# Loads of x re-ordered and spread over the run, a third buffer for the transposed softmax, and a new list order in an attention-and-MLP kernel

## The chip, the cores and the metric

The kernel runs on one core of one Trainium2 chip. The metric is the device time of a run in microseconds (us). Engines are named as in the profile: PE (TensorE), DVE (VectorE), ACT (ScalarE), POOL (GpSimd, which here mostly issues DMAs that convert FP32 to FP16 on the way) and SP (SyncE, which issues plain and transposing DMAs).

## What is computed

For each of 8 batches and 8 heads, 512 tokens x and 32 state vectors of width 64 attend to each other. Then all 8 x 544 rows go through an MLP whose activation is s·relu(h)² + b.

```python
scores = x @ state^T / 8;  a  = softmax(scores);   xread = a @ state     # 512 rows
scores2 = state @ x^T / 8; a2 = softmax(scores2);  sread = a2 @ x        #  32 rows
rows = concat(xread, sread) of all heads            # (8*544, 512)
r = relu(rows @ w_in)                               # (.., 2048)
out = (s*r*r + b) @ w_out                           # (.., 512)
```

All inputs and the output are FP32.

## The kernel before, in words

**Softmax.** Per batch, state and x are needed transposed (`stT`, `xT`). T holds the scores of all heads (`T_mm`, 16 small matmuls into two PSUM banks). ACT takes their exponential E (`E_exp`, L540). A matmul with a block matrix of ones gives the sums D over the 32 states (`D_mm`), and ACT forms 1/D as a logarithm and an exponential (L559, L566). The product a = E/D (L573) is the weight of xread. For sread, E is scaled by the row sums (`a2_mul`, L612), transposed by two DMAs to `aT` (`aT_dma`, L621) and multiplied with x (`V_mm`); the result goes through another transposing DMA to `srdT` (`sr_dma`, L651).

**First MLP matmul.** xread itself is never formed. M = stateᵀ-blocks times w_in is built per batch in four chunks of 512 columns (`M_mm`, eight small matmuls into two banks each, then two casts, L310 on ACT or L312 on DVE), and h = aᵀM gives 128 of the 2048 hidden rows in two matmuls of 512 columns (`h_mm`). There are 16 such f per batch. ReLU is on ACT (L779) or DVE (L771), the square on DVE (L785). h has two PSUM buffers.

**Second MLP matmul.** Batch 0 uses o = g·w_out directly, in 512-wide matmuls. Batches 1 to 7 use a Strassen-like scheme of seven products per batch in 256-wide matmuls, for which DVE forms differences of g (`pd`, L801 to L812) and of w_out (`u`, L860 to L866). DVE scales each product into an output tile (L928, L1024), and POOL or SP stores it (L934, L1036). The sread rows of all batches come last (`h_sr`, `osr`).

**Transposes.** Batches 0 to 2 (`NB_HW = 3`) transpose x and the state on PE with an identity, and DVE copies the result from PSUM. Batches 3 to 7 use transposing DMAs on SP for x (`dma_xT`, L462, four per batch) and one for the state (L446).

**Loads.** x of batch 0 comes as FP32 in four parts through SP (L248) and is cast by ACT. Everything else big is loaded on POOL with conversion, in the order of the string `SEQ` (L403), where wi and wo are quarters of w_in and w_out:

```python
SEQ = "wi0 x1 wi1 stf1 wo0 wi2 wo1 wi3 wo2 wo3 x2 sb x3 x4 x5"
```

x1 to x5 are whole batches. x of batches 6 and 7 comes in quarters of two heads each, with an earliest planned time from 62 us on. The first load waits for the identity through a small copy on POOL (`gate`, L402). A load issues only when the one eight places earlier has landed.

**Order.** No scheduler of the compiler is used. `Plan` holds a list of all operations, with an engine (or two to choose from) and a cost, a key, what each needs, and buffers. `Plan.order` walks through planned time and takes, on each free engine, the ready operation of the lowest key; that fixes the order of instructions on each engine. The keys are formed from the constants in `K`. While nothing is ready on PE, filler matmuls on the tile `warm` are placed until 14 us. `after` is an earliest planned time only: on the chip an instruction waits for what it needs and for those before it on its engine, not for a time.

Of the kernel before, what the change touches and what calls it, by code (L numbers as in the profile page):

```python
# [13 lines left out]
class Plan:  # L14
# [13 lines left out]
    def order(self, filler, fill_until, ready):  # L28
# [25 lines left out]
        mode, channel, log, now, done_n = False, 7.0, [], 0.0, 0  # L54
        times = []

# [15 lines left out]
        while done_n < len(ops):  # L72
            for e in free_at:
# [29 lines left out]
                if best is None:  # L103
                    fill = 0.43 if now < 7.0 else 0.22
                    if e == "PE" and now < fill_until and not any(since[i] < now + fill for i in cand[e]):
                        free_at[e] = now + fill
                        times.append(free_at[e])
                        log.append((now, len(log), "PE", filler, "warm", free_at[e]))
                    continue
# [13 lines left out]
                if land is not None:  # L123
                    kind, span = land
                    if kind == "load":
                        done = max(channel, end + 2.0) + span
                        channel = max(channel, done)
                    elif kind == "tp" and now < channel - 4.0:
                        end, done = now + 4.0, now + 9.0
                    else:  # L130
                        done = end + span
# [25 lines left out]
def kernel(  # L157
# [66 lines left out]
    nc.vector.memset(warm, 0.0)  # L224
    ident16 = konst.tile([P, P], FP16, name="ident16")
    ident_dr = nc.inline_tensor(np.eye(P, dtype=np.float16), name="ident_const")
    bones_np = np.kron(np.eye(4), np.ones((Ns, Ns))).astype(np.float16)
    bones16 = konst.tile([P, P], FP16, name="bones16")
    bones_dr = nc.inline_tensor(bones_np, name="bones_const")
    st_v = state.rearrange("b (g hf) j d -> (hf j) (b g) d", g=NG)  # L230
    NB_HW = 3
    stf = konst.tile([P, NG, D], FP32, name="stf")
    stf1 = konst.tile([P, (NB_HW - 1) * NG, D], FP32, name="stf1")
    stf2 = konst.tile([P, (B - NB_HW) * NG, D], FP32, name="stf2")
    xf = [upool.tile([P, H // 2, SCH * D], FP32, name=f"xf_{i}", tag="u") for i in range(2)]
    x0_v = x[0].rearrange("h (q c) d -> q h (c d)", q=P)

    def xf_part(i):
        return xf[i // 2][:, 2 * (i % 2) : 2 * (i % 2) + 2]
# [6 lines left out]
    nc.scalar.dma_start(stf, st_v[:, 0:NG, :])  # L246
    for i in range(4):
        nc.sync.dma_start(xf_part(i), xf_heads(x0_v, i))  # L248
    nc.scalar.dma_start(bones16, bones_dr.ap())
# [5 lines left out]
    s_bc = konst.tile([P, 1], FP32, name="s_bc")  # L255
    b_bc = konst.tile([P, 1], FP32, name="b_bc")
# [6 lines left out]
    st16 = konst.tile([P, B * NG, 2, D], FP16, name="st16")  # L263
    xn = {}
    xn[0] = xpool.tile([P, H, SCH, D], FP16, name="xn_0", tag="xn")

    def cast_x0(eng, i):
        eng(
            xf_heads(xn[0], i).rearrange("p h c d -> p h (c d)"),
            xf_part(i),  # L270
        )

    def cast_st(eng, src, n0, n):
        for k in range(2):
            eng.tensor_copy(st16[:, n0 : n0 + n, k, :], src)

    def late_dma(dst, src):


        nc.gpsimd.memset(dst, 0.0)  # L280
        nc.sync.dma_start(dst, src)

    K = dict(
        h1=4.4, hs=0.6, M0=-5.6, M1=0.9, T1=0.0, x2=24.6, T2=23.7, D2=27.2, M2=35.3, V0=27.7, V1=21.3, u=12.3,
        us=5.1, pd1=12.5, o0=13.1, o2=23.0, w=26.2, r=0.5, T=-9.8, D=3.1, Mb=6.4, V=8.6, S=3.6, S0=0.1, E=-0.5,
        L=-6.2, a4=-4.7, Mc=1.5, pd=13.4, solo=2.0, hsr=-4.1, Ssr=0.0,
# [3 lines left out]
    stTd = konst.tile([P, (B - NB_HW) * NG, P], FP16, name="stTd")  # L290
# [17 lines left out]
    def copy_on(e, dst, src):  # L308
        if e == "ACT":
            nc.scalar.copy(dst, src)  # L310
        else:
# [5 lines left out]
            "a40": 2, "a41": 2, "M": 2, "aT": 2, "a20": 2, "a21": 2, "sr": 4, "g": 8, "pd": 7,  # L317
# [16 lines left out]
    def cast_x0(i):  # L334
        def fn(e):
            copy_on(
                e,
                xf_heads(xn[0], i).rearrange("p h c d -> p h (c d)"),
                xf_part(i),
# [4 lines left out]
    def cast_st(e, src, n0, n):  # L344
        for k in range(2):
            copy_on(e, st16[:, n0 : n0 + n, k, :], src)

    add(DV(0.4), -30, lambda e: cast_st(e, stf, 0, NG), ["stf"], [("st", 0)])
    for i in range(4):
        add(  # L350
            (DV(0.35), AC(0.5)),
            -29 + i,
            cast_x0(i),
            [("xf", i)],
            [("x", 0, i)],
            [("u", f"xf{i // 2}"), ("xn", "x0")],
        )


    def load(key, dur, span, fn, makes, bufs=(), after=0.0):  # L360
        add(("POOL", dur), key, fn, [], makes, bufs, ("load", span), after=after)
# [21 lines left out]
    def load_x(b, h0=0, h1=H):  # L383
        def fn(e):
            if h0 == 0:
# [8 lines left out]
    def late(dst, src):  # L394
        def fn(e):
            nc.gpsimd.memset(dst, 0.0)
# [4 lines left out]
    gate = konst.tile([P, 2], FP16, name="gate")  # L401
    nc.gpsimd.tensor_copy(gate, ident16[:, 0:2])  # L402
    SEQ = "wi0 x1 wi1 stf1 wo0 wi2 wo1 wi3 wo2 wo3 x2 sb x3 x4 x5"  # L403
    seq = [(t,) if t in ("stf1", "sb") else (t[:-1], int(t[-1])) for t in SEQ.split()]
    for n, it in enumerate(seq):
        key = -40 + n
        if it[0] == "wi":
            load(key, 0.8, 4.2 if it[1] == 0 else 2.8, load_wi(it[1]), [it], after=3.4)
        elif it[0] == "wo":
            load(key, 0.8, 2.8, load_wo(it[1]), [it], after=3.4)  # L410
        elif it[0] == "x":
            b = it[1]
            load(
                key, 0.9, 2.9 if b == 1 else 3.9, load_x(b),
                [("x", b, i) for i in range(4)], [("xn", f"x{b}")], after=3.4,
            )
        elif it[0] == "stf1":
            load(key, 0.3, -3.0, late(stf1, st_v[:, NG : NB_HW * NG, :]), [it], after=3.4)
        else:
            load(key, 0.15, 0.1, late(s_bc, moe_s.to_broadcast((P, 1))), [("s",)], after=3.4)  # L420
            load(key + 0.1, 0.15, 0.1, late(b_bc, moe_b.to_broadcast((P, 1))), [("b",)], after=3.4)

    def load_stf2(e):
        nc.gpsimd.tensor_copy(stf2[:, 0, 0:2], wo[3][:, 0, 0:2])
        nc.sync.dma_start(stf2, st_v[:, NB_HW * NG :, :])

    add(("POOL", 0.3), -21, load_stf2, [("wo", 3)], [("stf2",)], (), ("side", 4.0))
    n1 = (NB_HW - 1) * NG
    add(
        DV(0.4), 0, lambda e: cast_st(e, stf1, NG, n1),  # L430
        [("stf1",)], [("st", 1), ("st", 2)],
    )
    add(
        ("POOL", 1.7), -19, lambda e: cast_st(e, stf2, NB_HW * NG, (B - NB_HW) * NG),
        [("stf2",)], [("st", 3)],
    )
    for k in range(8):
        b, i = 6 + k // 4, k % 4
        load(
            40 + 2 * k, 0.5, 1.0, load_x(b, 2 * i, 2 * i + 2),  # L440
            [("x", b, i)], [("xn", f"x{b}")], after=62.0 + 2.5 * k,
# [3 lines left out]
    def dma_stT(e):  # L445
        nc.sync.dma_start_transpose(  # L446
            stTd, st16[:, NB_HW * NG :].rearrange("p n k d -> p (n k d)")
        )

    add(("SP", 1.5), 18, dma_stT, [("st", 3)], [("stT", b) for b in range(NB_HW, B)], land=("tp", 3.0))  # L450

    def xT_of(b, h):
        if b < NB_HW:
# [3 lines left out]
    def dma_xT(b, i):  # L457
        def fn(e):
            if "xT" not in A[b]:
                A[b]["xT"] = apool.tile([P, H, 2, P], FP16, name=f"xT_{b}", tag="xT")  # L460
                A[b]["stT"] = stTd[:, (b - NB_HW) * NG : (b - NB_HW + 1) * NG]
# [7 lines left out]
    def stT_mm(b):  # L469
        def fn(e):  # L470
            A[b]["stTps"] = att_ps([P, NG, P], FP16, f"stTps_{b}")
            for g in range(NG):
                mm(
                    A[b]["stTps"][:, g, :],
                    st16[:, b * NG + g].rearrange("p k d -> p (k d)"),
# [6 lines left out]
    def stT_copy(b):  # L482
        def fn(e):
            A[b]["stT"] = apool.tile([P, NG, P], FP16, name=f"stT_{b}", tag="stT")
            copy_on(e, A[b]["stT"], A[b]["stTps"])
# [17 lines left out]
    def xT_copy(b, i):  # L503
        def fn(e):
            if i == 0:
                A[b]["xT"] = apool.tile([P, 2, 4, 2, P], FP16, name=f"xT_{b}", tag="xT")
            copy_on(e, A[b]["xT"][:, i], A[b][f"xTps{i}"])
# [3 lines left out]
    def st_T(b, g, q, m):  # L511
        h = head_of(g, q)
        return A[b]["stT"][64 * m : 64 * m + 64, h // 4, 32 * (h % 4) : 32 * (h % 4) + 32]
# [102 lines left out]
    def aT_dma(b, g):  # L616
        def fn(e):
            a = A[b]
            if "aT" not in a:
                a["aT"] = apool.tile([P, NG, SCH, P], FP16, name=f"aT_{b}", tag="aT")  # L620
# [41 lines left out]
    for b in range(B):  # L662
        if b < 2:
            kT = kD = kx = -10 if b == 0 else K["T1"]
            kM = [8 * c + (K["M0"] if b == 0 else K["M1"]) for c in range(4)]
# [9 lines left out]
        if b < NB_HW:  # L675
            stps = ("att", f"stps{b}")
            stT_b = [("stT", f"stT{b}")]
            add(PEt(0.13), kx, stT_mm(b), [("st", b), "ident"], [("stps", b)], [stps] + stT_b)
            add(DV(0.2), kx, stT_copy(b), [("stps", b)], [("stT", b)], [stps] + stT_b)
            for i in range(2):  # L680
# [3 lines left out]
                add(  # L684
                    (DV(0.62), AC(1.1)) if b == 9 else DV(0.62), kx + 0.1 * i, xT_copy(b, i),
                    [("xTps", b, i)] + ([("xT", b, 0)] if i else []), [("xT", b, i)], [ps, xT_b],
                )
        else:
            stT_b = []
# [440 lines left out]
```

The softmax here doesn't subtract the row's maximum and nothing guards it: scores larger than these inputs give would overflow.

## Time and profile before

| | |
|---|---|
| median of 8 runs | 213.84 us (213.21 to 214.06) |
| the profiled execution | 213.53 us |
| its span, first to last instruction | 211.4 us |
| busy PE, DVE, ACT, POOL in the span | 204.0, 175.1, 132.7, 37.0 us |
| granted PE clock | 0.998 |
| moved by DMA | 24.05 MB, mean 114 GB/s |
| first h matmul, last matmul starts | 13.79 us, 207.8 us |

The page lists busy time by engine and in 40 slices of the span, the chain of work that ended last, and the groups of instructions. Busy PE time can overlap, because matmuls are pipelined: a 512-wide h matmul is listed with 379 ns, but the next one follows after 0.215 us. The chain and the timeline give start, length and what released an instruction; "x8" means eight instructions merged.

### The profile page before, as it was taken

Reading aid. Unit: us, or ns where it says so; the run is one execution under the profiler, and the core shown is the slowest. Engines: PE = TensorE matmul, PEld = TensorE weight load, DVE = VectorE, ACT = ScalarE, POOL = GpSimd, SP = SyncE. Lnnn points to the kernel's source line nnn. Section 1 sums busy time; section 2 is a strip of 40 time slices with the busy share of each in tenths; the row PEclk is TensorE's granted clock in tenths of the full one; section 3 lists DMA queues with packets and bytes.
Section 4 is the critical chain, followed back from the end, with each engine's and each line's share of the span. In section 5 each row is a group of like instructions: output and inputs, shape, how many; then the busy total and the mean of one; then the engine's idle time right before and its main releaser. Section 6 shows DMA issues by size and latency. Waiting matters only on the chain.

```text
span 211.4 us, 4963 instructions
## 1 busy us (share of the span) xinstructions
PE 204.0 (96%) x1976; PEld 132.6 (63%) x1976; DVE 175.1 (83%) x412; ACT 132.7 (63%) x288; POOL 37.0 (18%) x60
## 2 busy tenths in 40 slices
PE   5998999999999999999999999999999999999993
PEld 1542333544557676667766776677676777888882
DVE  1358999999988869999988998899989988697652
ACT  4579997696375965796478657974697444632200
POOL 5733100040125261012101200111111111110000
PEclk9999999999999999999999999999999999999999
DMA  6999999999479994544064211321132111211142
GB/s 193 195 199 172 193 205 199 183 155 229 111 151 143 116 295 75 118 107 87 26 127 104 83 50 53 67 89 54 50 59 99 53 50 39 70 50 50 35 143 74
DMA packets 41463, 24.05 MB, mean 114 GB/s; under 512 B 25824, under 2 KB 39648, under 8 KB 41440
## 3 DMA queue, kind: packets, MB, share of 16 engines
q0 software_dynamic: 13840, 15.21, 36.2%
q1 hardware_dynamic: 27040, 8.40, 23.6%
q8 instruction: 15, 0.25, 0.5%
q10 hardware_dynamic: 560, 0.13, 0.3%
q14 instruction: 8, 0.07, 0.1%
HBM read 17.37 MB, written 8.91 MB: 124 GB/s over the span
## 4 chain that ended last, share of the span: by engine, by line
PE 90%; ACT 6%; DMA 2%; issue 0%; DVE 0%; SPq 0%
PE o L209 49%; PE h L209 25%; PE Mps L209 4%; PE h_sr L209 3%; PE osr L209 3%; ACT g L779 2%; PE xTps L209 2%; DMA xf<-in_x_dram 2%; PE D L209 2%; ACT M L310 1%; PE V L209 1%; ACT E L540 1%; PE T L209 1%; ACT D L559 1%; ACT R L566 1%
## 5 line engine op out<-in xcount | busy, mean ns | idle before, releaser
L779 ACT ACTIVATE g<-h 128x512 f16<-128x512 f32 x126 | 73.4, 601 | 41.3 <-PE h L209 41.1
L209 PE MATMUL h<-a,M 128*128 128x512 f16 x256 | 73.8, 379 | 0.6 <-ACT g L779 0.5
L785 DVE TENSOR_TENSOR g<-g 128x512 f16<-128x512 f16 x128 | 52.8, 421 | 4.3 <-ACT g L779 2.8
L209 PEld LDWEIGHTS <-pd 128*128 128x128 f16 x448 | 42.6, 98 | 20.0 <-issue 3.4
L209 PEld LDWEIGHTS <-g 128*128 128x128 f16 x400 | 39.0, 98 | 19.5 <-issue 0.2
L209 PE MATMUL o<-u,pd 128*128 128x256 f16 x336 | 45.9, 273 | 0.0
L209 PE MATMUL o<-wo,g 128*128 128x256 f16 (+1 forms) x288 | 45.5, 296 | 0.0
L1036 POOL DMA_DIRECT2D out_dram<-c x24 | 16.3, 681 | 103.8 <-DVE c L1024 100.9
L209 PEld LDWEIGHTS <-M 128*128 128x128 f16 x256 | 24.1, 98 | 13.2 <-issue 4.6
L310 ACT CAST M<-Mps 128x512 f16<-128x512 f32 x45 | 25.3, 595 | 7.1 <-PE Mps L209 7.1
L1024 DVE SCALAR_TENSOR_TENSOR c<-o,s_bc,bias_bc 128x512 f32<-128x512 f32 x28 | 21.0, 750 | 7.2 <-PE o L209 6.3
L801 DVE TENSOR_TENSOR pd<-g 128x1024 f16<-128x1024 f16 x28 | 19.2, 686 | 0.3
L1024 DVE SCALAR_TENSOR_TENSOR c<-o,s_bc,c 128x512 f32<-128x512 f32 x21 | 15.7, 750 | 1.8 <-PE o L209 1.6
L209 PE MATMUL o<-wo,pd 128*128 128x256 f16 x112 | 16.2, 273 | 0.0
L209 PE MATMUL o<-u,g 128*128 128x256 f16 x112 | 15.5, 273 | 0.0
L312 DVE CAST M<-Mps 128x512 f16<-128x512 f32 x19 | 13.0, 686 | 2.0 <-PE Mps L209 1.9
L773 ACT ACTIVATE g_sr<-h_sr 128x256 f16<-128x256 f32 x16 | 6.1, 384 | 10.5 <-PE h_sr L209 10.3
L540 ACT ACTIVATE E<-T 128x256 f16<-128x256 f32 x32 | 11.9, 390 | 1.0 <-PE T L209 0.9
L812 DVE TENSOR_TENSOR pd<-g,pd 128x512 f16<-128x512 f16 x28 | 11.8, 421 | 0.4
L387 POOL DMA_DIRECT2D xn<-in_x_dram x13 | 10.4, 820 | 8.9 <-DMA wi<-in_moe_w_in_dram 4.5
L810 DVE TENSOR_TENSOR pd<-g,pd 128x512 f16<-128x512 f16 x28 | 11.7, 418 | 0.0
L559 ACT ACTIVATE D<-D 128x512 f32<-128x512 f32 x16 | 9.6, 601 | 1.6 <-PE D L209 1.5
(71 smaller groups left out, 162.9 us busy)
## 6 DMA issues: line engine op xcount, KB each, us to landing
out_dram<-c POOLq DMA_DIRECT2D x24, 256.0 KB, 2.5
xn<-in_x_dram POOLq DMA_DIRECT2D x5, 512.0 KB, 22.1
wi<-in_moe_w_in_dram POOLq DMA_DIRECT2D x4, 512.0 KB, 14.1
wo<-in_moe_w_out_dram POOLq DMA_DIRECT2D x4, 512.0 KB, 20.1
xf<-in_x_dram SPq DMA_DIRECT2D x4, 256.0 KB, 3.7
out_dram<-osb POOLq DMA_DIRECT2D x4, 256.0 KB, 4.1
xn<-in_x_dram POOLq DMA_DIRECT2D x8, 128.0 KB, 4.5
out_dram<-c SPq DMA_DIRECT2D x4, 256.0 KB, 2.5
```

The source lines that it names most:

```text
L209: return nc.tensor.matmul(out, lhsT, rhs, start=start, stop=stop, tile_position=tp, is_transpose=is_transpose, skip_group_check=True,)
L310: nc.scalar.copy(dst, src)
L312: ENG[e].tensor_copy(dst, src)
L540: nc.scalar.activation(a["E"][g][:, 256 * m : 256 * m + 256], a["T"][m][:, g, :], AF.Exp, scale=scale, accum_out=a["rs"][:, g, m : m + 1],)
L559: nc.scalar.activation(A[b][f"D{g}"], A[b][f"D{g}"], AF.Ln)
L779: nc.scalar.activation(g_of(name, f), OSB["h", name, f], AF.Relu)
L785: ENG[e].tensor_mul(g_of(name, f), g_of(name, f), g_of(name, f))
L801: nc.vector.tensor_tensor(pd[:, :, 0:2], g4[:, :, 1:2, :].to_broadcast((P, 2, 2, t)), g4[:, :, 0:4:3, :], ALU.subtract,)
L810: nc.vector.tensor_tensor(pd[:, :, 2], g4[:, :, 3], pd[:, :, 0], ALU.subtract)
L812: nc.vector.tensor_tensor(pd[:, :, 3], g4[:, :, 2], pd[:, :, 2], ALU.subtract)
L1024: nc.vector.scalar_tensor_tensor(t, src, s_bc, add, ALU.mult, ALU.add)
L1036: ENG[e].dma_start(dst[:, rows:SCH:2, hD * h : hD * h + hD], SN[b, name])
```

## The change

- x of batch 1 is loaded like that of batch 0: four FP32 parts through SP, ahead of all weights, cast by ACT and DVE. The POOL gate waits for the third part of x of batch 0.
- The order on POOL is wi0 wo0 wi1 wi2 wo1 wo2 wi3 wo3 x2 x3. x3 waits for `aT` of batch 1. x of batches 4 to 7 comes in quarters, planned from 57, 78, 100 and 122 us on.
- x of batch 2 is transposed by DMA (`NB_T = 2`). The state of four batches is loaded and transposed on PE in one block (two blocks for batches 0 to 3), with rows in another order; the sread ReLU restores the order in two instructions instead of one. The state of batches 4 to 7 is transposed by DMA.
- `aT` has three buffers instead of two.
- The block matrix of ones is written by DVE memsets instead of loaded. s and b are loaded into four partitions and spread by DVE.
- Constants in `K` and the planner's costs are new: transposing DMAs on SP are planned with their own landing times (8.3 us for xT, 12.9 and 7.4 for aT) and a longer time while loads are running. ReLUs of batches 2 to 7 may go to DVE.

```diff
-        mode, channel, log, now, done_n = False, 7.0, [], 0.0, 0
+        mode, channel, log, now, done_n = False, 9.35, [], 0.0, 0
+        for k in range(9):
+            log.append((free_at["PE"], len(log), "PE", filler, "warm", free_at["PE"] + 0.43))
+            free_at["PE"] += 0.43
...
-                    elif kind == "tp" and now < channel - 4.0:
-                        end, done = now + 4.0, now + 9.0
+                    elif kind == "tp" and e == "SP" and now < channel + 4.0:
+                        done = end + max(span, min(8.0, 6.0 - 0.75 * (now - channel)))
+                        channel = max(channel, now + 2.0) + 1.1
...
-    bones_dr = nc.inline_tensor(bones_np, name="bones_const")
+    nc.vector.memset(bones16, 0.0)
+    for q in range(4):
+        nc.vector.memset(bones16[Ns * q : Ns * q + Ns, Ns * q : Ns * q + Ns], 1.0)
...
+    for i in range(4):
+        nc.sync.dma_start(xf_part(1, i), xf_heads(x_v[1], i))
...
     def load_x(b, h0=0, h1=H):
         def fn(e):
+            if b == 3:
+                nc.gpsimd.tensor_copy(gate, A[1]["aT"][:, :, 0, 0])
...
-    nc.gpsimd.tensor_copy(gate, ident16[:, 0:2])
-    SEQ = "wi0 x1 wi1 stf1 wo0 wi2 wo1 wi3 wo2 wo3 x2 sb x3 x4 x5"
+    nc.gpsimd.tensor_copy(gate, xf_part(0, 2)[:, 0, 0:2])
+    SEQ = "wi0 wo0 wi1 wi2 wo1 wo2 wi3 wo3 x2 x3"
...
-    for k in range(8):
-        b, i = 6 + k // 4, k % 4
+    for k in range(16):
+        b, i = 4 + k // 4, k % 4
         load(
             40 + 2 * k, 0.5, 1.0, load_x(b, 2 * i, 2 * i + 2),
-            [("x", b, i)], [("xn", f"x{b}")], after=62.0 + 2.5 * k,
+            [("x", b, i)], [("xn", f"x{b}")], after=[57.0, 78.0, 100.0, 122.0][b - 4] + 2.5 * i,
+            needs=[("x", 3, 0)],
         )
...
+    def spread_sb(e):
+        nc.vector.tensor_copy(sb_rows.rearrange("p (k j) -> p k j", k=2), sb_in[:, 0:2].unsqueeze(2).to_broadcast((P, 2, 32)))
+        nc.vector.transpose(sb_cols, sb_rows)
...
-                a["aT"] = apool.tile([P, NG, SCH, P], FP16, name=f"aT_{b}", tag="aT")
+                a["aT"] = apool.tile([P, NG, SCH, P], FP16, name=f"aT_{b}", tag="aT", bufs=3)
...
-                    OSB["h", name, f].rearrange("p (i b j) -> p i j b", i=2, b=B // 2),
+                    hps[:, 0:P].rearrange("p (b r j) -> p j r b", r=4, b=B // 2),
+                    AF.Relu,
+                )
+                nc.scalar.activation(
+                    g[:, P:].rearrange("p (j b) -> p j b", b=B // 2),
+                    hps[:, P:].rearrange("p (b j) -> p j b", b=B // 2),
```

In the instruction lists this gives 32 instead of 48 transposes of x on PE, 8 instead of 6 of the state, 23 instead of 24 fillers, 51 instead of 45 M casts on ACT and 13 instead of 19 on DVE, and 24 instead of 20 transposing DMAs for x.

## The prediction

> **What bounds the kernel now.** I read the page first: the sliced busy rows, to see where TensorE (PE) is not full.
>
> ```profile
> PE   5998999999999999999999999999999999999993
> ...
> ACT  4579997696375965796478657974697444632200
> ...
> PEclk9999999999999999999999999999999999999999
> ```
>
> A slice is 5.3 us. PE is full from slice 6 on, at the full granted clock; ACT is the busiest other engine only in slices 2 to 6. So from about 30 us on only PE work taken away helps; before that there may be idle time. The table by stage says the same with numbers (PE busy is the first figure after the length, ACT busy the fourth pair, GB/s last).
>
> ```profile
> 13.79:28.57 14.78, 13.49 (x117) 5.53 (x116) 12.66 (x33) 13.11 (x32) 3.66 (x6) 1.00 1.18 189
> 28.57:44.00 15.43, 15.29 (x130) 6.88 (x129) 15.25 (x39) 12.13 (x30) 0.87 (x3) 1.00 1.37 193
> ...
> 62.00:78.00 16.00, 16.00 (x170) 11.38 (x169) 13.29 (x30) 11.83 (x28) 6.49 (x10) 1.00 1.27 177
> 78.00:178.00 100.00, 100.00 (x1034) 68.97 (x1032) 90.84 (x205) 67.88 (x143) 12.78 (x19) 1.00 0.31 75
> ```
>
> PE busy overstates work at the start, since it counts filler matmuls on `warm` and overlapping tails. I therefore count PE by what one instruction delays the next, read from the chain rows: an h matmul 0.215 us (x4 in 0.86), a 256-wide o matmul 0.109 (x8 in 0.87), a transpose 0.056 (x8 in 0.45), a group of eight M matmuls about 0.30, sixteen T 0.28, two D 0.43, a V group 0.35. Over the whole kernel these make 189.5 us of useful PE time; the last matmul ends at 207.8, so 18.2 us are lost. Where: before the first h matmul at 13.79 stand 16+2 transposes, 16 T, 2 D and 8 M, 2.0 us of work, so 11.8 us lost. From there to 28.57 the timeline of PE holds 28 h (6.05), 12 512-wide o (2.6), 18 transposes (1.0), 5 M groups (1.5), 16 T and 2 D (0.7): 11.85 of 14.78, 2.9 lost. 0.5 goes until 44, and 3.0 in the remaining 164 us, at the changes between small and full tiles.
>
> What holds PE between 16 and 26 us is seen in the chain of waits:
>
> ```profile
> 15.82 0.45 PE h L209 x2
> 16.27 0.02 issue
> 16.29 0.60 ACT g L779
> 16.89 0.97 ACT M L310 x2
> 17.86 0.57 ACT E L540 x3
> ...
> 20.32 0.60 ACT R L566
> 20.92 0.50 ACT D L559
> ...
> 24.49 0.48 ACT M L310
> 24.96 0.51 ACT g L779
> 25.47 0.04 issue
> 25.52 0.61 PE h L209 x2
> ```
>
> ACT is the bound here: the softmax of batch 1 (four E, two D, two R, about 3.5 us) stands in the same stretch as the ReLUs and M casts of batches 0 and 1. It does so because x of batch 1 comes behind wi0. The loads on POOL show when: each row issues when the load eight places earlier has landed.
>
> ```profile
> 10.71 0.75 POOL L376 DMA_DIRECT2D wo<-in_moe_w_out_dram  x1 [1.35 <-DMA wi<-in_moe_w_in_dram]
> 14.14 0.89 POOL L387 DMA_DIRECT2D xn<-in_x_dram  x1 [2.69 <-DMA xn<-in_x_dram]
> 16.69 0.88 POOL L387 DMA_DIRECT2D xn<-in_x_dram  x1 [1.52 <-DMA wi<-in_moe_w_in_dram]
> 19.28 0.88 POOL L387 DMA_DIRECT2D xn<-in_x_dram  x1 [1.71 <-DMA wo<-in_moe_w_out_dram]
> ```
>
> So wi0 landed by 10.7, x1 by 14.1, wi1 by 16.7, wo0 by 19.3: about 2.6 us for each weight piece.
>
> **Part 1, the start.** x of batch 1 moves in front of the weights. Between 3 and 5 us the DMA engines moved 335 GB/s; 2.1 MB of x in FP32 and 0.16 MB of state and identity take 6.7 us from about 2.4, so the last quarter lands near 9.6 and the third near 5.3. The gate copy on POOL now waits for that third quarter, not for the identity: wi0 issues at 5.5 instead of 2.83, and lands behind x at 9.3 + 2.6, about 12.0 (11.4 if it overlaps x without loss; 13.4 if issue to landing stays at the 7.9 us of before). Then wo0 14.6, wi1 17.2, wi2 19.8, wo1 22.4, wo2 25.0, wi3 27.6, wo3 30.2. In exchange the batch 1 casts, transposes and T use engines that sat idle: of the first 13.79 us DVE is busy 4.6 and ACT 8.2.
>
> I walk the new order of each engine with old durations and 0.2 us from PE to a reader. ACT casts x0 until 6.7 and one x1 quarter, copies half of xT, then E at 8.2 to 9.5, D and R until 11.6. DVE casts three x1 quarters by 9.7 (as each lands), q by 10.0, copies xT of batch 1 (0.69 each, a between) and ends the second a at 12.05. PE starts M at 12.1 with wi0, then T and M of batch 1, whose two PSUM banks wait for the first casts at 13.2; first h at 13.6, about as before. But 3.6 us of useful work stand before it (32+4 transposes, 32 T, 2 D, 2 M groups), so 10.0 are lost instead of 11.8: a gain of **1.8**.
>
> Then ACT: E of batch 1 until 14.4, ReLUs mixed with D and R until 17.7. PE waits from 16.0 to 17.2 for wi1, the one new wait; behind it stand M, four o and all h. After that I find h and o alternating at ACT's pace of 0.49 us per ReLU or cast, and the tenth h of batch 0 ends at 27.45 with 15.6 useful, 11.85 lost. So 1.85 is lost in this stretch, against 2.9: **1.1** gained. From there to 40.4 the walk loses 0.65 against 0.5: **0.15** given back.
>
> New small items: the state of four batches is transposed in two blocks (8 transposes, not 6, 0.1 us); its strided copy of 128x512 lies between the 0.29 of 128x256 and the 0.69 of 128x1024, before wi0 lands; five bones memsets of at most 0.1 sit in DVE's 3.5 us wait for the state. s and b come as 2x4 elements, not 2x128: at 20 to 21 us before, when they moved, the DMA fell to 58 GB/s, so about 1 us of loading is saved, which I leave as reserve. The spreading copy and transpose on DVE have no row in before; between 0 and 0.5 us (if they wait for the late s and b, with M casts and squares queued behind); I take 0.
>
> **Part 2, batch 2 by transposing DMA.** 16 PE transposes leave (0.89) and two state ones come: **0.78** gained on PE where it is full. Two DVE copies of 0.69 leave too. Its four transposing DMAs wait on SP behind those of the transposed softmax. Under load in before these took 1.3 to 2.1 us each to issue and up to 9.8 to land; x2 lands near 33, so xT is there near 45 and T stands at PE's 48.7. Covered by 3 us.
>
> x of batch 3 now waits on POOL for aT of batch 1 and stands behind two stores of batch 0. These need DVE's output near 41, so x3 issues near 42 and lands by 47 (by 52 at the 9.9 us that the slowest transfer under load took). Behind it on POOL are the stores of batch 0's other rows and x4; its transposing DMAs wait on SP for aT of batch 2 anyway (from about 51) and end by 61, T of batch 3 comes at 68: 0, with 7 us of cover.
>
> **Part 3, fewer spare microseconds.** In before T of batch 3 comes 14 us of PE work ahead of its first h; in the new order 5.3, and 4.8 for batch 2. From T at 41.44 to the last a at 47.2 the old trace needs 5.8, with 1.0 of ReLU and cast between. I find 5.2 and 4.65 for the new lists: it just fits. Bounds: 0 and 1.0 for both; I take **0.4** lost.
>
> **Part 4, x of batches 4 to 7 in quarters.** Batches 6 and 7 were so before; 4 and 5 are new. Eight issues of 0.78 replace two of 0.88 on POOL, which is 18% busy. Trace first: the old quarters took 4.5 us to land in the median, 8.2 at most, and the stage 62 to 78 us that held them lost no PE time. The Trainium skill, DMA: Bandwidth & Descriptors, section Rules for kernel authors, speaks against it: coalesce small transfers, each costing about 2 us fixed (its section on the anatomy of one DMA). By that rule six more transfers cost 12 us if they stood on the path; by the row, 0. I take the row: T of such a batch stands 15.5 us of PE work after the output step whose store precedes the last three quarters on POOL, and they need 0.75 (DVE output) + 0.65 + 1.45 (issues) + 4.5, then about 5.2 for the transposing DMAs, 12.6. Margin 2.9.
>
> The third buffer for aT frees a wait that the trace does not show: 0. The sr ReLU becomes two 128x128 instructions: 384 ns was one; ACT is 8.5 of 22 us busy there, and PSUM comes free within the 1.3 us that two h_sr and their o take: 0. The tail after the last matmul is unchanged.
>
> **Sum.** -1.8 - 1.1 + 0.15 - 0.78 + 0.4 = -3.1. The profiled execution took 213.53 (span 211.4 and 2.1 around it): 210.4. It lies 0.3 below the median 213.84, so against the median: **210.7**.
>
> **Rivals.** (a) Loads bind: wi0 at 13.4 and all behind it 1.4 later. The first h waits, the gain before it shrinks to 0.4, and of the ACT stretch 0.4 stays: 213.84 - 0.4 - 0.4 - 0.78 + 0.3 = 212.6. For it: DMA is near 190 GB/s all along. Against: before, the first h came 3 us after wi0. (b) The new lists leave no holes: half of the 1.85 lost goes, part 3 costs nothing, the saved 1 us of loading shortens the wait for wi1: 209.0. Against: ACT stays near full. (c) Slower: a quarter behind an output store lands late. Each us beyond the margin stops PE for batches 4 to 7, with all h and o behind T. To undo 3.1 and end over 0.4 slower each must stall 0.9: landings of 8.3 us where the median is 4.5; at 9 it gives 213.84 - 3.1 + 4 x 1.6 = 217. For it: one old quarter took 8.2. Against: it did so amid four transposes, and once. (d) The change doesn't do what it says: ACT's work is only moved, the 1.8 and 1.1 come back as waits of h for ACT before 40 us, and part 3 eats 0.4 of the 0.78: 213.5, no change.
>
> **Chances.** Forecast 0.62 (209.8 to 211.7); (a) 0.14; (b) 0.12; (c) 0.06; (d) 0.06. Within 0.2% (0.43 us) is what a measurement can't tell from no change. (a) to its upper end and (d) share out as faster 0.88, same 0.06, slower 0.06. For 8 in 10 the range takes in (a) and (b): 208.9 to 212.7.
>
> **What would show it.** First h near 13.6 with E of batch 1 starting before 14; wi0 landing near 12; only short ACT pieces in the chain between 16 and 27; PE gapless from 30; 32 transposes of x; T of batches 4 to 7 not released by a DMA. Wrong if wi0 lands after 13, if PE idles at T or at h of batches 2 and 3, or if the chain holds DMA after 40 us.

## The result and the profile after

The changed kernel takes 211.79 us in the median (210.54 to 213.07, 11 runs) where the kernel before takes 213.86 beside it (213.21 to 214.76, 32 runs): ratio 0.9904, interval 0.9888 to 0.9921. That is 2.07 us less; 3.1 were predicted. The profiled execution took 212.49, span 210.7, mean granted clock 0.990. Ratios leave out runs more than 1.5% above the fastest of the same kernel, which concerns only the kernel below whose weights are not held back for x.

The page, in 40 slices: PE busy, ACT busy, and the granted clock of PE.

```profile
PE   7896999999999999999999999999999999999993
...
ACT  4896899832996698959596859675977554116500
...
PEclk9997899999999999999999999999999999999999
```

In the first slice PE is fuller than before (7 against 5), but only by fillers: nine stand there instead of five. The second has 8 against 9, and the fourth (16 to 21 us) has 6 against 8. In the fourth and fifth the clock is not full; in before it was. The timeline of PE shows why (start, length, what; in brackets the idle time ahead and what ended it):

```profile
14.24 1.04 PE L213 MATMUL h<-a,M 128*128 128x512 f16 x4
...
15.58 1.09 PE L213 MATMUL h<-a,M 128*128 128x512 f16 x4
18.57 0.41 PE L213 MATMUL Mps<-wi,stT 64*32 64x512 f16 x8 [1.90 <-DMA wi<-in_moe_w_in_dram]
18.91 1.89 PE L213 MATMUL o<-wo,g 128*128 128x512 f16 x4
20.60 1.87 PE L213 MATMUL h<-a,M 128*128 128x512 f16 x4
```

The first h stands at 14.24. PE then idles 1.90 us for wi1. The M group that ends the wait still runs at its usual pace (0.34 us to the next instruction), but the eight 512-wide matmuls behind it take about 0.43 us each instead of 0.215. The table by stage gives the clock (PE busy is the first figure after the length; the clock is the third from the end):

```profile
16.00:20.00 4.00, 2.10 (x14) 0.72 (x13) 3.74 (x10) 3.35 (x7) 0.00 (x0) 0.86 1.23 203
20.00:24.00 4.00, 4.00 (x27) 1.23 (x26) 2.04 (x6) 2.08 (x4) 0.19 (x1) 0.71 1.24 203
```

The chain of waits, which in before held pieces of ACT between 16 and 26 us, now holds the load and then PE alone:

```profile
7.67 10.86 DMA wi<-in_moe_w_in_dram
...
18.98 1.82 PE o L213 x4
20.80 1.67 PE h L213 x4
```

So the bound of this stretch has passed from ACT to the loads, and 3.4 us of PE at half clock add 1.7 us. From 36 us on PE has no gap, and no T of batches 4 to 7 waits for a DMA.

### The profile page after: what moved, and what is told of

It reads as the page before. It is cut to its first block, busy times and chain, and to the rows that moved or that the text cites. A ratio compares the mean times of both kernels' runs of the same rounds, so it can differ in the third digit from the quotient of the medians.

```text
span 210.7 us, 4984 instructions
## 1 busy us (share of the span) xinstructions
PE 203.0 (96%) x1961; PEld 131.7 (63%) x1961; DVE 173.9 (83%) x415; ACT 138.2 (66%) x311; POOL 40.5 (19%) x65
## 4 chain that ended last, share of the span: by engine, by line
PE 88%; DMA 7%; ACT 1%; POOL 1%; SPq 0%; DVE 0%; issue 0%
PE o L213 48%; PE h L213 26%; DMA wi<-in_moe_w_in_dram 5%; PE Mps L213 4%; PE h_sr L213 3%; PE osr L213 3%; DMA xf<-in_x_dram 2%; PE V L213 1%; PE D L213 1%; PE T L213 1%; ACT g L804 1%; PE wsum_ps L213 0%; SPq L255 0%; POOL wi L361 0%; POOL wo L371 0%; DVE c_sr L1049 0%
## 5 line engine op out<-in xcount | busy, mean ns | idle before, releaser
L213 PE MATMUL h<-a,M 128*128 128x512 f16 x256 | 74.8, 383 | 0.0
L810 DVE TENSOR_TENSOR g<-g 128x512 f16<-128x512 f16 x128 | 51.4, 420 | 5.9 <-ACT g L804 4.5
L213 PE MATMUL o<-wo,g 128*128 128x256 f16 (+1 forms) x288 | 46.3, 300 | 0.0
L305 ACT CAST M<-Mps 128x512 f16<-128x512 f32 x51 | 28.7, 594 | 7.3 <-PE Mps L213 7.0
L1049 DVE SCALAR_TENSOR_TENSOR c<-o,sb_cols,bias_bc 128x512 f32<-128x512 f32 x28 | 21.0, 749 | 6.1 <-PE o L213 5.5
L1049 DVE SCALAR_TENSOR_TENSOR c<-o,sb_cols,c 128x512 f32<-128x512 f32 x21 | 15.8, 751 | 5.7 <-PE o L213 5.2
L548 ACT ACTIVATE E<-T 128x256 f16<-128x256 f32 x32 | 11.9, 385 | 4.9 <-PE T L213 4.9
L213 PE MATMUL o<-wo,pd 128*128 128x256 f16 x112 | 15.0, 273 | 0.0
L384 POOL DMA_DIRECT2D xn<-in_x_dram x18 | 13.9, 811 | 0.4 <-DMA wi<-in_moe_w_in_dram 0.4
L837 DVE TENSOR_TENSOR pd<-g,pd 128x512 f16<-128x512 f16 x28 | 11.8, 422 | 0.5
L793 ACT ACTIVATE g_sr<-h_sr 128x128 f16<-128x128 f32 x16 | 4.4, 278 | 11.8 <-PE h_sr L213 11.8
L835 DVE TENSOR_TENSOR pd<-g,pd 128x512 f16<-128x512 f16 x28 | 11.8, 420 | 0.3
L574 ACT ACTIVATE R<-D 128x512 f16<-128x512 f32 x16 | 9.6, 597 | 0.5
```

Source lines behind the costliest of these rows:

```text
L213: return nc.tensor.matmul(out, lhsT, rhs, start=start, stop=stop, tile_position=tp, is_transpose=is_transpose, skip_group_check=True,)
L384: nc.gpsimd.dma_start(out=xn[b][:, h0:h1].rearrange("p h c d -> p h (c d)"), in_=x[b, h0:h1].rearrange("h (q c) d -> q h (c d)", q=P),)
L548: nc.scalar.activation(a["E"][g][:, 256 * m : 256 * m + 256], a["T"][m][:, g, :], AF.Exp, scale=scale, accum_out=a["rs"][:, g, m : m + 1],)
L574: nc.scalar.activation(A[b][f"R{g}"], A[b][f"D{g}"], AF.Exp, scale=-1.0)
L810: ENG[e].tensor_mul(g_of(name, f), g_of(name, f), g_of(name, f))
L835: nc.vector.tensor_tensor(pd[:, :, 2], g4[:, :, 3], pd[:, :, 0], ALU.subtract)
```

## The experiments

Theory A after this profile: what is missing of the forecast lies in the wait for wi1, by its length and by the low clock behind it, which comes in some executions and not in others. Rival B: the low clock is chance, and the gain was mis-sized elsewhere. All kernels are the changed kernel with one edit, unless said otherwise. Below, a "low-clock run" is one with a mean granted clock under 0.995. "Loss" is the time of PE minus its useful time, counted as in the prediction. A "filler" is a matmul whose result nothing reads.

**Fillers in the wait for wi1.**

```diff
     for step in steps:
+        if step[4] == (("Mps", 0, 1),):
+            for _ in range(8):
+                filler("PE")
```

> The changed kernel with eight filler matmuls (8 x 0.216 = 1.7 us) put on PE just before the M matmuls that wait for wi1; they fill the wait, they don't shorten it. Theory A: PE sat idle for 1.9 us at 16.5 us, its clock then fell to half for about 3 us, and not in every run. Then the fillers keep the clock: no matmul pair at 0.43 us per 512 columns after 18.5, the loss at the tenth h of batch 0 falls from 14.8 to about 13.3, the profiled time falls by 1.5, the median from 211.8 to about 211.0, and the spread of 2.5 us between runs narrows to about 1. Rival B: the clock falls for a reason that has nothing to do with this wait (total power, chance): median 211.8 and the same spread.

Measured: 211.72 (211.24 to 214.25, 10 runs), ratio 0.9917 (0.9892 to 0.9943). One low-clock run of ten, the one at 214.25. In its profile the clock stays at 1.0 and the loss grows by only 0.20 over the M, o and h behind the wait, against 1.72 in the profile of the changed kernel; but the loads came later here (wi0 at 13.03, wi1 at 19.23). The 211.0 that theory A expected was missed: the nine runs at full clock average 211.71. So the fillers are not shown to shorten this kernel.

**The first four o ahead of that M.**

```diff
+    steps.insert(at[(("Mps", 0, 1),)], steps.pop(at[(("o", 0, 0, 0),)]))
```

> The changed kernel with the first four o matmuls of batch 0 (needing wo0, landed at 15.2, and four squares, done near 17.5) moved on PE ahead of the M matmuls that wait for wi1 (18.5); every other list is the same. Theory A: the idle stretch shrinks from 1.9 to about 1.0 and 0.86 us of work is done in it, and the shorter gap costs less clock: 211.8 - 0.9 - up to 0.8 = 210.1 to 210.9. Rival B (clock unrelated): 210.9. Rival C: ACT is the bound until 30 us, so that work moved ahead on PE only waits later: 211.8.

Measured: 211.36 (210.75 to 212.05, 5 runs), ratio 0.989 (0.987 to 0.991), no low-clock run. The interval overlaps with the changed kernel's: a gain over it is not shown, and 211.36 lies between the 210.9 of B and the 211.8 of C, so that none of the three is picked out.

**Batch 2 back on PE** (the planner then also shifts its lists).

```diff
-    NB_T = 2
+    NB_T = 3
```

> The changed kernel with x of batch 2 transposed on PE again (16 matmuls, two DVE copies) and no transposing DMAs for it; the planner's lists shift with it. The prediction's term: 0.89 us of PE work come back where PE is full, 211.8 + 0.9 = 212.7. Rival: the place where they stand has PE time to spare (ACT-bound), 211.8.

Measured: 213.58 (212.71 to 214.52, 14 runs), ratio 0.9994 (0.9978 to 1.0011): about 1.8 slower than the changed kernel. The useful time of PE rises from 188.73 to 189.62, the 0.89 of sixteen transposes. The rest is loss: in the profile 0.45 more than the mean of the changed kernel's between the tenth h and 40 us, with this wait of a transpose for x2, which DMA transposes keep off PE's list,

```profile
35.27 1.07 PE L213 MATMUL xTps<-ident,xn 128*128 128x128 f16 x16 [0.49 <-DMA xn<-in_x_dram]
```

and 0.6 more later. This fits a worth of 0.78 or more for Part 2. The lists moved with the edit, though, so the 1.8 is not Part 2's alone, and the 0.89 is counted from the transposes, not measured apart. Two of the fourteen runs were low-clock; the profile, at full clock, has waits of 1.34 and 1.20 us for wi0 and wi1.

**x of batches 4 and 5 whole.**

```diff
-    for k in range(16):
+    for b in (4, 5):
+        load(
+            24 + 16 * (b - 3), 0.9, 3.9, load_x(b),
...
+    for k in range(8, 16):
```

> The changed kernel with x of batches 4 and 5 loaded whole, one DMA each, behind the same stores; batches 6 and 7 in quarters as before; the lists of ACT, DVE and SP change in a few places. The prediction's term: the quarters cost nothing, 211.8 within 0.3. Rival by the rule on small transfers: two DMAs instead of eight save some us of landing on the way to T of batches 4 and 5, under 211.3. Rival the other way: the whole load can't start its first transposes early and collides with stores, over 212.2.

Measured: 210.92 (210.61 to 213.53, 7 runs), ratio 0.9916 (0.9875 to 0.9957). Three low-clock runs at 212.5 to 213.5, the other four at 210.61 to 210.92. In its profile PE idled nearly as long for wi1 as in the changed kernel's, yet the clock held:

```profile
18.54 0.41 PE L213 MATMUL Mps<-wi,stT 64*32 64x512 f16 x8 [1.73 <-DMA wi<-in_moe_w_in_dram]
18.88 1.04 PE L213 MATMUL o<-wo,g 128*128 128x512 f16 x4
```

So a wait of this length may or may not take the clock down. The four runs at full clock lie some 0.7 below those of the changed kernel (210.80 against 211.50 in the mean), which looked like a gain by fewer loads; a later run put that to the test.

**The changed kernel again, with no edit,** on the chip of the next three.

> The changed kernel again, nothing altered, as the measure for the runs beside it. Theory A (the wait of PE for wi1 of 1.9 to 2.0 us sometimes takes the granted clock down for some 3 us behind it): about 211.5 in the runs with a clock of 0.995 or more, and about a third of the runs at 0.993 or less and 1.1 or more above those. Rival B (the low clock of the profiled execution was chance and has nothing to do with the wait): low-clock runs as rare here as in the kernels whose wait is filled.

Measured: 211.61 (210.91 to 213.36, 6 runs), ratio 0.9907 (0.9874 to 0.994). No low-clock run of six: theory A's "a third" was missed here. wi0 landed at 13.13, the first h stood at 14.73, and the profile shows a second wait for the loads:

```profile
29.75 0.41 PE L213 MATMUL Mps<-wi,stT 64*32 64x512 f16 x8 [0.80 <-DMA wi<-in_moe_w_in_dram]
```

**o first, and four fillers in each of the two waits left.**

> The first four o matmuls of batch 0 stand before the M that waits for wi1, and four matmuls on a tile that nothing reads (0.85 us together) stand before these o's and four more before that M, in the two waits that are left. Theory A: no run below a clock of 0.995, a median 0.3 to 0.6 below the unchanged kernel's (211.1 to 211.4), mostly by the low-clock runs that are missing. Rival B: the median within 0.2 of the unchanged kernel's, since the fillers stand in time that was lost anyway, and low-clock runs as often as there. Rival C (the fillers end after their data have landed and delay it): 0.3 to 0.8 above the kernel with the o's first alone.

Measured: 211.74 (211.06 to 212.47, 6 runs), ratio 0.9905 (0.9879 to 0.9931), no low-clock run. The median fits rival B (within 0.2 of the unchanged 211.61) and rival C (0.38 above the kernel with the o's first, though the intervals overlap). The profile shows what C describes: wi1 landed at 17.13 here, but the M that needs it came at 19.34, behind the o's and the fillers.

```profile
16.66 1.02 PE L213 MATMUL o<-warm 128*128 128x512 f16 x4
17.52 1.03 PE L213 MATMUL o<-wo,g 128*128 128x512 f16 x4
18.38 1.03 PE L213 MATMUL o<-warm 128*128 128x512 f16 x4
19.34 0.41 PE L213 MATMUL Mps<-wi,stT 64*32 64x512 f16 x8
```

**wo1 loaded before wi1, so that the wait becomes long,** without and with twenty fillers in it.

```diff
+    steps.insert(at[(("wi", 1),)], steps.pop(at[(("wo", 1),)]))
```

> wo1 is loaded before wi1, all else as in the changed kernel, so that wi1 lands where wo1 did, near 21 instead of 18.5, and the wait of PE in front of the M that needs it grows from 1.9 to about 4.5 us. Theory A: the wait costs its own 2.5 us and takes the clock down in every run or nearly every run, 1.1 to 2.0 more, so 215 to 216, clock 0.985 to 0.993. Rival B (no tie between wait and clock): the 2.5 alone, 214.0, clocks as in the unchanged kernel. Rival C (the time is made up later, since the ACT stretch behind waits anyway for later weights): 212.5 to 213.5.

> As the kernel with wo1 before wi1, but with twenty matmuls on a tile that nothing reads, 4.3 us together, in that long wait. Theory A: no low clock, so 1.1 to 2.0 below the one without them. Rival B: equal to it within 0.3, or 0.2 to 0.5 above it where the fillers end after wi1 has landed.

Measured: bare 215.74 (215.41 to 215.97, 4 runs), ratio 1.0096 (1.0067 to 1.0124), all four low-clock; filled 214.33 (213.59 to 216.16, 20 runs), ratio 1.0034 (1.0017 to 1.005), two low-clock runs, at 215.82 and 216.16. The bare wait and what follows it:

```profile
21.45 0.41 PE L213 MATMUL Mps<-wi,stT 64*32 64x512 f16 x8 [4.50 <-DMA wi<-in_moe_w_in_dram]
21.79 1.89 PE L213 MATMUL o<-wo,g 128*128 128x512 f16 x4
23.47 1.90 PE L213 MATMUL h<-a,M 128*128 128x512 f16 x4
```

and the filled one, with the same o at full clock:

```profile
17.71 4.48 PE L213 MATMUL o<-warm 128*128 128x512 f16 x20
22.12 0.41 PE L213 MATMUL Mps<-wi,stT 64*32 64x512 f16 x8
22.46 1.04 PE L213 MATMUL o<-wo,g 128*128 128x512 f16 x4
```

Same loads, same order of useful work, M even 0.67 later in these two profiles: yet 1.41 us faster. For a wait of this length rival B falls: all four bare runs had a low clock and 2 of 20 filled ones. Rival C falls too: even filled, the kernel is 2.7 slower than with wi1 in its place (211.61), so little of the wait was made up later.

**Both likely improvements together:** x4 and x5 whole, o first, fillers.

> Two edits on the changed kernel together: x of batches 4 and 5 whole again (two loads for eight), and the first four o matmuls of batch 0 before the M that waits for wi1, with four fillers in each of the two waits. Theory A (the fewer loads are worth some 0.6 by themselves, as the kernel with x4 and x5 whole showed in its runs at full clock, and the filled wait keeps the clock up): no run under a clock of 0.995, median 210.6 to 211.0, so 0.7 to 1.1 below the changed kernel. Rival B (the fewer loads are worth nothing, the difference was chip or chance): 211.3 to 211.7, as the kernel with the o's first and fillers alone.

Measured: 212.07 (211.74 to 212.74, 6 runs), ratio 0.9909 (0.9882 to 0.9936), no low-clock run. Theory A's 210.6 to 211.0 was missed: the gain of the whole loads did not come again. The median lies above rival B's 211.3 to 211.7 as well. No version here is shown to beat the changed kernel.

**aT with two buffers, all lists the same.**

> The third buffer for aT is taken away; the instruction lists of all engines are the same. Theory A (the trace shows no wait for that buffer; worth 0): within 0.2 of the changed kernel. Rival B (the third buffer is what lets the transposes of aT run early enough under the load of the start): 0.5 to 1.5 slower, with PE waiting at V or at M of batches 2 to 4.

Measured: 211.6 (211.3 to 212.65, 4 runs), ratio 0.9891 (0.9855 to 0.9927). That is within 0.2 of the changed kernel, as theory A said. Four runs don't resolve half a microsecond, but the profile has none of the waits of rival B: PE is busy 8.00 of 8.00 us from 44 to 52, from 52 to 60 and from 60 to 68, and 32.00 of 32.00 from there to 100. One low-clock run of four, the 212.65. Since its lists are the changed kernel's own, its profile counts as a third one of that kernel below.

**The weights not held back for x of batch 0.**

```diff
-    nc.gpsimd.tensor_copy(gate, xf_part(0, 2)[:, 0, 0:2])
+    nc.gpsimd.tensor_copy(gate, ident16[:, 0:2])
```

> The weights are held back for the identity only, as before the change, instead of the third part of x of batch 0: wi0 issues near 2.8 instead of 6.0 and shares the DMA engines with x of batches 0 and 1. Theory A (the start is bound by the sum of the bytes, and the order in which they land decides little): wi0 lands 0.5 to 1.5 earlier, near 11 to 12, the last part of x1 about 1 to 2 later, first h within 0.5 of the changed kernel, wi1 0.5 to 1 earlier, total 0 to 0.6 faster. Rival B (x1 late puts the exponentials of batch 1 back into the stretch that ACT bounds): first h no earlier, and 0.4 to 1.2 slower in all.

Measured: 215.77 in the median (211.88 to 217.93, 20 runs), 14 of them low-clock. The nine runs that count in its ratio, 0.9985 (0.996 to 1.0011), average 213.56, still 1.8 above the changed lists on the same chip (two aT buffers, 211.79 in the mean), more than either theory had. The low clock is not all of it: the six runs at full clock average 213.20, the three of the other 211.50. The profiled execution is a long one (216.82), so only its order of events is used. wi0 landed at 11.85, hardly earlier; the last part of x1 at 15.55 instead of 9.90; and M of batch 0 stands behind the transposes of x1 in PE's list:

```profile
10.52 0.66 PE L213 MATMUL T<-xT,stT 64*32 64x256 f16 x8 [1.17 <-ACT E L548]
11.11 1.23 PE L213 MATMUL xTps<-ident,xn 128*128 128x128 f16 x8
...
16.06 0.61 PE L213 MATMUL xTps<-ident,xn 128*128 128x128 f16 x4 [1.65 <-DVE xn L307]
16.46 2.34 PE L213 MATMUL o<-warm 128*128 128x512 f16 x5
18.73 0.63 PE L213 MATMUL Mps<-wi,stT 64*32 64x512 f16 x8
```

The clock fell here as well, and for longer: it stands at half from 11.22 to 21.46, although the longest wait of PE between its first matmul and there is 1.17.

So the order in which the same bytes land counts, with lists made for one order. Holding the weights back is a working part of the change; that x1's lateness is what costs the 1.8 is read from a long execution and not shown apart.

**The kernel before once more,** for a second profile.

> The kernel before once more, for a second profile of its start. If the landing of the weights scatters there as it does in the changed kernel (wi0 from 11.8 to 13.9 in six profiles), its first h stands between 13.3 and 15, and one profile of each kernel tells the difference at the start only to about 1; if before is steady, first h lies within 0.2 of 13.8.

Measured: 213.98 (one run). wi0 landed at 11.52, 1.1 later than in its first profile (10.42), and the first h moved from 13.79 to only 13.90:

```profile
12.04 0.41 PE L209 MATMUL Mps<-wi,stT 64*32 64x512 f16 x8
12.38 1.68 PE L209 MATMUL o<-warm 128*128 128x512 f16 x7
13.90 1.03 PE L209 MATMUL h<-a,M 128*128 128x512 f16 x4
```

So before had cover against a late wi0. In the changed kernel's three profiles wi0 landed at 12.44, 13.13 and 13.31 and the first h followed 1.80, 1.60 and 1.60 later: there is none. Of the two branches expected, the steady one held: before's first h doesn't scatter with its loads.

## Why the prediction was right, and where it was mis-sized

The direction was right, and so was the claim that the start and the PE work taken away make the gain; the sum was 1.0 too large. 211.79 lies 0.09 above the forecast's own range of 209.8 to 211.7, on the side of rival (a), and inside the wider range of 8 in 10. The table sets each term beside what two profiles of before and three of the changed lists (the two of the changed kernel and that with two aT buffers) show. Figures are PE's loss in us, each at the end of the same piece of work.

| step | predicted | before, 2 profiles | after, 3 profiles | difference of means |
|---|---|---|---|---|
| up to the first h | -1.8 | 11.8, 11.9 | 10.64, 11.13, 11.31 | -0.8 |
| to the tenth h of batch 0 | -1.1 | 2.9, 3.2 | 4.18, 3.01, 2.31 | +0.1 |
| to 40 us (before: 44) | +0.15 | 0.5, 0.5 | 0.53, 0.76, 0.60 | +0.1 |
| the rest | +0.4 | 3.0, 3.0 | 2.84, 2.83, 2.82 | -0.2 |
| useful PE time | -0.78 | 189.51 | 188.73 | -0.78 |

Together -1.5. The time outside the span fell too, from 2.1 to 1.8 us in all these executions, which nothing in the prediction covers and no run explains. That makes -1.8 in the means of the profiled executions (213.76 to 211.92); the medians say -2.07. So two terms were 1.0 and 1.2 too hopeful, and the number came out as near as it did because 0.6 in the rest and 0.3 outside the span, neither foreseen, went the other way. That part was luck.

- **Part 1, first h: the term "wi0 lands about 12.0" was mis-sized.** It landed at 12.96 in the mean of the three, between the 12.0 taken and the 13.4 given as the far bound, and in two of the three after 13, which the prediction had named as a sign of being wrong. The first h was put 1.6 behind it and stands 1.67 behind it (at 14.24, 14.73 and 14.91 instead of 13.6). So the missing 1.0 of this step is wi0's lateness. Some 0.6 of it is a late issue. The third part of x of batch 0 was put at 5.3, but the gate that waits for it ran at 5.89, 6.17 and 5.89, and wi0 issued at 6.02, 6.30 and 6.02 instead of 5.5:

```profile
5.89 0.19 POOL L392 CAST gate<-xf 128x2 f16<-128x2 f32 x1 [5.45 <-DMA xf<-in_x_dram]
6.02 0.91 POOL L361 DMA_DIRECT2D wi<-in_moe_w_in_dram  x1
```

  The other 0.35 is the way from issue to landing, 6.42, 6.83 and 7.29 us instead of 6.5. In the two longer ones two of the sixteen DMA engines were late: fourteen had landed by 12.32 and 12.03, the last at 13.13 and 13.31. Two slips of its working did no harm: 6.7 us from 2.4 make 9.1 for the end of x, not 9.3 or 9.6 (9.90, 9.82 and 9.53 were measured), and the 7.9 us from issue to landing in before are 7.6 by the landing itself, which turns 13.4 into 13.1. The step also missed that before's first h hardly depends on wi0, so that cover was given up.
- **The ACT stretch: the term "PE waits from 16.0 to 17.2 for wi1", 1.2 us, was right in kind and mis-sized in consequence.** The idle time was 1.90, 0.92 and 1.48; the first is in the timeline above, the others are

```profile
18.29 0.41 PE L213 MATMUL Mps<-wi,stT 64*32 64x512 f16 x8 [0.92 <-DMA wi<-in_moe_w_in_dram]
19.02 0.41 PE L213 MATMUL Mps<-wi,stT 64*32 64x512 f16 x8 [1.48 <-DMA wi<-in_moe_w_in_dram]
```

  What was absent from the sum is the clock. In the first profile it cost 1.7, which makes 4.18 out of some 2.5. In the second, wi3 came late by another 0.8. In the third, where neither happened, 2.31 were lost against 1.85 predicted. ACT did leave the chain, as the prediction said: in the third profile the chain from 19 to 28.9 us is PE alone. But of the gain of 1.1 only 0.7 was there in that profile, and nothing in the other two. This is rival (a) in part, though its 212.6 for all runs was too high.
- **The low clock.** Low-clock runs with a bare wait of about 1 to 2 us: 4 of 12, 0 of 6, 3 of 7, 1 of 4 and 2 of 14 (changed kernel, the same again, whole x4 and x5, two aT buffers, batch 2 back on PE), 10 of 43; with the wait filled or o moved into it: 1 of 10, 0 of 5, 0 of 6, 0 of 6, 1 of 27; with a bare 4.5 us: 4 of 4; with that filled: 2 of 20. None of 78 runs of before beside the experiments. For the long wait the tie is shown; for waits under 2 us it is a tendency over several chips. In the changed kernel's first set, low-clock runs averaged 212.62 and the others 211.50. With a third of the runs low, that is about 0.4 in the mean, against the 1.0 that is missing. The profile shows what such a fall costs: 3.41 us at half clock (third figure from the end) in the changed kernel, and the same behind the bare 4.50 us wait.

```profile
15.47:18.88 3.41, 1.51 (x14) 0.48 (x11) 3.34 (x8) 3.28 (x7) 0.00 (x0) 1.00 1.24 207
18.88:22.30 3.42, 3.42 (x16) 1.01 (x8) 1.78 (x4) 1.20 (x3) 0.00 (x0) 0.50 1.22 199
...
21.81:25.23 3.42, 3.42 (x16) 1.01 (x8) 1.82 (x5) 1.18 (x2) 0.00 (x0) 0.50 1.22 219
```

  In both the fall comes 0.3 to 0.4 us after PE has started again, and half of 3.41 is the 1.7: in these two profiles the price did not grow with the wait. The Trainium skill, TensorE: Matmul & The Clock Gate, section HAM oscillation — how this bites in real kernels, gives as the rule that PE should have no idle gaps above about 3.4 us. The 4.50 us row agrees. The 1.90 us row does not: the clock fell there at a little over half that gap, though not in every execution, and in the kernel whose weights are not held back it fell behind a wait of 1.17. By the rule the wait costs 1.9, by the row 3.6.
- **27.45 to 40.4 us (+0.15)** and **Part 2 (-0.78)** held. Putting batch 2 back cost 1.8, which fits 0.78 as a lower bound of its worth in these lists.
- **Part 3 (+0.4)** did not occur: M, h and o of batches 2 and 3 show no gap in the changed kernel's profile. The bound of 0, which rival (b) also had, was the right end.
- **Part 4 (0)** held, as far as the runs resolve it. Whole x4 and x5 gave 210.92 once and, with the o's first and fillers, 212.07 once. The prediction's estimate from the rule on small transfers (the Trainium skill, DMA: Bandwidth & Descriptors, section Rules for kernel authors) was 12 us for the six further ones if they stood on the path; nothing of that size appears, and PE is full in the stages where those of batches 4 and 5 land (8.00 of 8.00 us from 60 to 68, and from there to 100 as this row shows).

```profile
68.00:100.00 32.00, 32.00 (x323) 21.91 (x321) 28.75 (x68) 25.92 (x58) 7.96 (x12) 1.00 0.59 117
```

- **aT's third buffer (0)** held by its own run. Rival (c), the late quarter, and rival (d), work only moved, are ruled out by the full PE and by the 2.07; rival (b), no holes at the start, by the losses in the table.

What stays open: why one or two of the sixteen DMA engines land so late, what decides whether a wait under 2 us takes the clock down, and the 0.3 outside the span. On the second, the profiles show only that the length of the wait alone doesn't decide (a fall behind 1.17 and 1.90, none behind 1.34, 1.48 and 1.73), and that the half clock lasted 3.41 us or three times that (10.24). A start that depends less on wi0's landing was not tried.

## What to carry to other kernels

When a change takes one engine off the path at the start, ask what is next and how much its own time scatters: here the loads were next, with wi0 landing anywhere from 11.8 to 13.9 in eleven profiles of the changed kernel and its close variants, and cover that had absorbed this scatter was gone. Price a new PE wait by its length and by the matmuls behind it at half clock (1.7 us here), and fill it if it is long; for waits under 2 us no gain by fillers was shown here. Fillers must end before the data can land, or they become the wait. One profile, or a few runs on one chip, can show a gain of 0.6 us that the next kernel doesn't repeat.

## What was not expected of the hardware

- A PE idle for 1.90 us ran at half clock for 3.41 us, from 0.3 us after its return on, with 512-wide matmuls at 0.43 instead of 0.215 us; another, idle for 1.73 us, did not; a third fell to half clock for 10.24 us behind a wait of 1.17.
- wi1's last DMA engine landed 0.85 us after the fifteenth in the changed kernel's profile, 1.5 (17.72 and 19.23) in that with fillers, 0.8 (15.61 and 16.41) in before's.
- With wi1 loaded behind wo1, useless matmuls in a 4.5 us wait made the kernel 1.41 us faster.
- Loading the weights 3.1 us sooner, together with x, delayed the last part of x1 by almost 6 us (9.90 to 15.55) and brought wi0 only 0.6 us (12.44 to 11.85).
